# A convolution stem's gradients on one core: eight sums of raw steps of x made during the forward convolution and kept in DRAM, and one more split leaf

## The chip, the cores and the metric

The kernel runs on one core of a Trainium2 chip. Its time is the device time of one execution in microseconds (us); lower is better. TensorE (PE) multiplies, VectorE (DVE) and ScalarE (ACT) work on elements, GpSimd (POOL) sets small areas, and SyncE (SP) issues nearly all DMAs from one queue, in order. Each engine carries out its own instructions strictly in the order in which they were written down, so one that waits holds up all behind it on its engine.

## The reference, cut to what matters

```python
B, T, D, K = 2, 16000, 256, 31          # stride 2, L = 7985 output rows
h = einsum('blc,cd->bld', x[:, 0:2*L:2, :], w[0]) + ... + (the same for taps 1 to 30)
mu, var = mean and variance of h over l
out = gelu((h - mu) / sqrt(var + 1e-5) * gn_gamma + gn_beta)      # tanh form
# returned: out, and the gradients of x, w, gn_gamma, gn_beta for grad_out
```

Everything is bf16 in and out. There are three large products: the forward convolution, the gradient of x, and the gradient of w (31 taps of 256 x 256, each a sum over both batches and all 7985 rows).

## The kernel before

**Fewer multiplications by sums.** All three convolutions are split by Karatsuba's rule, several levels deep: in place of the four products of two halves with two halves, three products are made, with sums or differences of the operands, and combined afterwards. A, C_ and B_ name the first half, the second half, and their combination. DVE makes the operands' sums and differences; PE's work becomes less and DVE's more. Where the innermost level is split too, a "leaf" becomes three smaller products.

**Stages.** The order of the program is F0 and F1 (forward convolution, batch 0 and 1, `forward`), G0 and G1 (gradient of x, `input_grad`), W (gradient of w, `weight_grad`). The forward convolution of a batch takes x in four quarters c = 0 to 3; each is turned by DMA into the one buffer XT (`x_load`) and worked on in three branches, in the order B_, A, C_. `forward` is a generator: after each branch it yields (b, c, br), and the loop at the end of `conv_stem_kernel` adds other work there. In F0 that is `w2_part(c)`: a quarter of w's taps is turned by four DMA transposes into VR, five differences are made into VD, and nine stores of 256 KB put them into DRAM (vl) for the gradient of x. VR and VD lie at byte REG of the arena, 14336 bytes together. After batch 0's statistics, `gelu_batch(0, REG, ...)` takes a ring of buffers at the same place; its 16 units (`gelu_unit`, lines 947 to 986, five multiplications or additions on line 968 each) run beside F1 and have to be done before `e_comp(0, 0)` can make the input of G0.

**W.** `weight_grad` goes through nine combinations n = 0 to 8 (`COMBOS`: (A,A), (A,C), (A,B), (C,B), (B,B), (B,A), (B,C), (C,A), (C,C)) of the two outer levels. For each it needs four tiles of x (`x_tile`, 1 MB each, for two batches and two halves k3). A tile of (A,A), (A,C), (C,A) or (C,C) is one raw load; (A,B) and (B,B) are made in place from tiles that are there; (C,B), (B,A) and (B,C) each need two raw loads and one addition of 4096 elements per partition (`w_add`, line 1413). Then XSUM is made from each pair of tiles (also line 1413), a pair sum of it (`pair_x`, line 1508), differences of the gradient's tiles (`leaf_d`, line 1587; `pair_d`, line 1516), and the products: `w_pairs` and `w_single` in matmuls of 256 columns, `w_leaf` in matmuls of 512 (all on line 1447). A whole leaf is 64 matmuls of 512 columns. A leaf in the set `NODES` is split into 96 matmuls of 256 columns, for which DVE makes two pair sums, four pair differences and two PSUM additions (`w_both`, line 1540). `place` hands out the buffers for these from up to three sets; the set "late" shares its bytes with XR, the buffers of the second raw loads.

**What sets the order.** Every instruction is first only noted (`Plan.add`) with a duration and its reads and writes. `Plan.listing` then plays all engines and DMAs through and picks for each engine the instruction that is ready and has the earliest due time: that of its first user, or PE's time at its noting plus `slack`, shifted by the entry of its kind in the table `lead`. `hold` keeps an instruction back until PE has come to a given place, `look` says how far PE may pick ahead, `pads` spreads work with time to spare further from the DMAs it waits for. `PACE` gives the due times of the GELU units. The resulting order is then fixed in the program.

Lines used later: 561 (`tt` in `f_sums`), 551 (`w_sub`), 596 (`f_mm`, forward matmuls), 676 (`ve`), 680 (`ve_neg`), 1162 (`g_mm`, matmuls of the gradient of x), 1357 (`sub` in `d2_piece`), 415 and 420 (`load` and `turn`, all DMAs).

Of the kernel before, what the change touches and what calls it, by code (L numbers as in the profile page):

```python
# [11 lines left out]
BF16 = mybir.dt.bfloat16  # L12
ACT = mybir.ActivationFunctionType
ALU = mybir.AluOpType
# [6 lines left out]
A, B_, C_ = 0, 1, 2  # L21
# [17 lines left out]
class Plan:  # L39
# [3 lines left out]
    def __init__(self, tc):  # L43
# [9 lines left out]
        self.lead = {  # L53
            "F0 f_mm f_three_ac": -2.5,
            "F0 f_mm f_three_b": -4.0,
            "F0 f_mm pe_turn": 9.5,
            "F0 f_three_b f_first": 2.0,
            "F0 f_three_b forward": 2.5,
            "F0 keep f_first": 4.5,
            "F0 load load_w": -4.5,  # L60
            "F0 put x_first": -4.5,
            "F0 tt second": -1.0,
            "F0 tt third": -1.5,
            "F0 turn w2_part": 8.0,
            "F0 turn x_load": -3.5,
            "F0 ve f_first": -1.0,
            "F0 ve f_seed": -4.0,
            "F0 w_sub f_first": 2.0,
            "F1 f_mm f_leaf": -4.0,
            "F1 f_mm f_three_ac": -3.0,  # L70
            "F1 f_mm f_three_b": -9.5,
            "F1 f_three_b forward": 4.5,
            "F1 gelu_unit gelu_batch": 3.0,
            "F1 load gelu_unit": -2.0,
            "F1 tiny elem_finalize": 2.0,
            "F1 tiny fwd_stats": -11.5,
            "F1 tt f_sums": 1.5,
            "F1 tt gelu_unit": -4.0,
            "F1 tt second": -7.5,
            "F1 turn x_load": -3.0,  # L80
            "G0 e_comp conv_stem_kernel": -1.0,
            "G0 g_mm g_three_ac": 3.0,
            "G0 g_mm g_three_b": -3.0,
            "G0 g_three_b input_grad": 6.0,
            "G0 keep g_evac": -3.0,
            "G0 load dn_turn": 1.0,
            "G0 load e_load": 4.5,
            "G0 load gelu_unit": 2.0,
            "G0 load load_w2": 4.0,
            "G0 tiny elem_finalize": -8.5,  # L90
            "G0 tt first": -2.0,
            "G0 tt second": -9.0,
            "G0 turn gelu_batch": -7.0,
            "G0 w_sub load_w2": -8.0,
            "G1 e_comp conv_stem_kernel": 12.5,
            "G1 g_mm g_leaf": -4.0,
            "G1 g_mm g_outer": -1.5,
            "G1 g_mm g_three_ac": -4.0,
            "G1 keep g_evac": -10.5,
            "G1 load dn_turn": -11.5,  # L100
            "G1 load e_load": -2.5,
            "G1 load g_evac": 20.0,
            "G1 signed g_seed": -7.5,
            "G1 spread e_comp": -5.5,
            "G1 sub d2_piece": -7.5,
            "G1 tt first": 9.5,
            "G1 tt second": -5.5,
            "G1 tt third": -2.0,
            "G1 ve_neg g_seed": 11.5,
            "W keep w_keep": -2.0,  # L110
            "W keep weight_grad": 3.0,
            "W leaf_d weight_grad": -2.0,
            "W pair_x weight_grad": -1.5,
            "W turn out0_late": -7.0,
            "W ve w_done": 12.0,
            "W ve weight_grad": -3.5,
            "W w_add weight_grad": -2.0,
            "W w_add x_tile": 3.0,
            "W w_both weight_grad": 9.0,
            "W w_emit w_done": 7.5,  # L120
            "W w_mm w_leaf": -3.5,
            "W w_mm w_single": 0.5,
            "W w_pairs weight_grad": -2.5,
# [211 lines left out]
def conv_stem_kernel(  # L335
# [33 lines left out]
    dn_d = [dram.tile([NDR, D], BF16, name=f"dnd{b}") for b in range(NB)]  # L369
    pc_d = [dram.tile([P, 1024], FP32, name=f"pcd{k}") for k in range(4)]  # L370
# [1033 lines left out]
    NODES = {(0, A), (0, C_), (1, A), (1, C_), (3, A), (4, A), (6, A), (7, A), (7, C_), (8, C_)}  # L1404
# [16 lines left out]

    def x_tile(n, b, k3):
        i1, i2 = COMBOS[n]
        j = KEYS.index((b, k3))
        t = (XT_ if n % 2 else XS_)[j]
        if (i1, i2) in ((A, B_), (B_, B_)):
            w_add(t, t, XT_[j])
        else:
            ks = [(k1, k2) for k1 in raws[i1] for k2 in raws[i2]]
            x_raw(b, k3, *ks[0], t)  # L1430
            for k in ks[1:]:
                w_add(t, t, x_raw(b, k3, *k))
        return t
# [120 lines left out]
    def weight_grad():  # L1554
# [3 lines left out]
        def place(n):  # L1558
            ks = ("all",) + (("early",) if n < 2 else ()) + (("late",) if n not in (3, 5) else ())
# [98 lines left out]
    PACE = ((1385.0, 117.0), (191.0, 24.5))  # L1658
    fw = forward()
# [99 lines left out]
```

## Time and profile before

| | us |
|---|---|
| median of 3 runs | 1187.01 (1183.07 to 1188.23) |
| the profiled execution, its own time | 1189.54 |
| its span, first to last instruction | 1187.8 |
| PE busy / DVE busy / ACT busy | 1149.0 / 1047.6 / 570.0 |
| DMA queue of SP: bytes | 253.93 MB |

The profile shows one execution. "Idle before" in a group's row is the time its engine stood still just ahead of these instructions, with what ended it; in the rows in order of time the same stands in brackets. A matmul's own duration overlaps with the next one's, so PE's pace is read from stretches without a wait, not from the mean of one. The granted clock is 1.00 where PE runs at full speed. The DMA share is the mean busy share of 16 DMA engines; it can come out above 1.

### The profile page before, as it was taken

To read this page: it belongs to the slowest core of one execution; us is meant where nothing else is said; L and a number is where in the kernel's file an instruction comes from. 1 tells how busy PE (TensorE), PEld (TensorE's weight loads), DVE (VectorE), ACT (ScalarE), POOL (GpSimd) and SP (SyncE) were. 2 spreads that over 40 slices of the span, in tenths; PEclk is the share of its full clock that TensorE was granted. 3 is DMA by queue.
4 is the path that set the end of the run, shared out by engine and by line. 5 is a ranking of instruction groups with operands and counts; after the bars stand their busy time and mean duration, and the time that the engine had idled before them with its cause. 6 is when DMAs were issued, how large, how long until landed. Compare 5 with 4: busy or idle time off the path is not lost.

```text
span 1187.8 us, 19338 instructions
## 1 busy us (share of the span) xinstructions
PE 1149.0 (97%) x7739; PEld 763.5 (64%) x7796; DVE 1047.6 (88%) x1358; ACT 570.0 (48%) x873; POOL 18.9 (2%) x67
## 2 busy tenths in 40 slices
PE   5999999999999999999999999999999999989998
PEld 3888889777777964444444444444488656656685
DVE  7997898799999989999879997788889898777995
ACT  1254454788885578978884476433322212111200
POOL 0000000000000000000000000000000000000000
PEclk9999999999999999999999999999999999999999
DMA  9446949968986799567639998697998824986774
GB/s 212 73 115 122 200 121 182 205 146 204 204 209 124 270 353 252 167 225 186 221 115 292 270 329 265 161 318 266 317 235 266 271 90 151 359 300 198 239 219 140
DMA packets 334100, 255.17 MB, mean 215 GB/s; under 512 B 187500, under 2 KB 312682, under 8 KB 325738
## 3 DMA queue, kind: packets, MB, share of 16 engines
q1 hardware_dynamic: 333818, 253.93, 76.6%
q8 instruction: 61, 1.00, 0.3%
q14 instruction: 29, 0.24, 0.1%
q0 software_dynamic: 192, 0.00, 0.0%
HBM read 118.95 MB, written 89.62 MB: 176 GB/s over the span
## 4 chain that ended last, share of the span: by engine, by line
PE 46%; DVE 14%; DMA 6%; issue 4%; ACT 1%; SPq 0%; DVEq 0%; ACTq 0%
PE ps L1162 27%; PE ps L1447 15%; PE ps L596 4%; DVE arena L1413 3%; DMA arena<-in_x_dram 2%; DMA arena<-dnd 2%; DVE arena L1357 2%; DVE arena L1587 2%; DVE ps L676 1%; DVE arena L676 1%; DVE arena L1516 1%; DVE arena L1508 1%; DMA dnd<-arena 1%; DVE arena L1121 1%; DVE ps L1540 1%
## 5 line engine op out<-in xcount | busy, mean ns | idle before, releaser
L1162 PE MATMUL ps<-arena 128*128 128x512 bf16 x1974 | 429.7, 376 | 6.6 <-DVE ps L676 3.6
L596 PE MATMUL ps<-arena 128*128 128x256 bf16 (+4 forms) x3460 | 408.2, 281 | 17.8 <-DVE arena L551 7.1
L596 PEld LDWEIGHTS <-arena 128*128 128x128 bf16 x3460 | 338.1, 99 | 87.7 <-DVE arena L551 7.5
L1162 PEld LDWEIGHTS <-arena 128*128 128x128 bf16 x2016 | 197.3, 98 | 237.7 <-issue 6.8
L1447 PE MATMUL ps<-arena 128*128 128x256 bf16 (+1 forms) x2305 | 312.1, 298 | 10.5 <-DVE arena L1508 7.3
L1447 PEld LDWEIGHTS <-arena 128*128 128x128 bf16 x2320 | 228.1, 98 | 94.6 <-DVE arena L1508 8.7
L691 ACT ACTIVATE arena<-ps 128x1024 f32<-128x1024 f32 (+1 forms) x143 | 145.7, 1020 | 285.3 <-PE ps L1447 98.1
L561 DVE TENSOR_TENSOR arena<-arena 128x1087 bf16<-128x1087 bf16 (+3 forms) x211 | 175.5, 866 | 13.7 <-PE ps L596 12.4
L968 DVE TENSOR_TENSOR arena<-arena 128x1024 bf16<-128x1024 bf16 x160 | 107.0, 683 | 8.5 <-ACT arena L962 3.9
L1413 DVE TENSOR_TENSOR arena<-arena 128x4096 bf16<-128x4096 bf16 x38 | 86.3, 2284 | 20.8 <-DMA arena<-in_x_dram 19.5
L1121 DVE TENSOR_TENSOR arena<-arena 128x516 bf16<-128x516 bf16 (+3 forms) x176 | 83.6, 506 | 8.6 <-PE ps L1162 8.0
L676 DVE TENSOR_TENSOR ps<-ps,arena 128x1024 f32<-128x1024 f32 x60 | 73.1, 1224 | 7.9 <-PE ps L1447 4.5
L1357 DVE TENSOR_TENSOR arena<-arena 128x768 bf16<-128x768 bf16 (+3 forms) x112 | 65.4, 636 | 9.9 <-DMA arena<-dnd 4.7
L711 ACT ACTIVATE arena<-ps 128x512 bf16<-128x512 f32 (+1 forms) x64 | 36.9, 578 | 70.4 <-PE ps L596 67.9
L676 DVE TENSOR_TENSOR ps<-arena,ps 128x1024 f32<-128x1024 f32 x44 | 53.8, 1223 | 9.3 <-PE ps L1162 5.5
L1532 ACT COPY ps<-ps 128x256 f32<-128x256 f32 x54 | 19.3, 357 | 78.7 <-PE ps L1447 77.6
L1587 DVE TENSOR_TENSOR arena<-arena 128x2304 bf16<-128x2304 bf16 x36 | 47.4, 1348 | 4.8 <-PE ps L1447 4.8
L1516 DVE TENSOR_TENSOR arena<-arena 128x1024 bf16<-128x1024 bf16 x76 | 48.7, 682 | 1.6 <-DMA arena<-d2d 1.6
L551 DVE TENSOR_TENSOR arena<-arena 128x2048 bf16<-128x2048 bf16 (+1 forms) x52 | 49.8, 989 | 0.0
L958 DVE SCALAR_TENSOR_TENSOR arena<-arena 128x1024 bf16<-128x1024 bf16 x32 | 39.0, 1219 | 11.3 <-ACT arena L956 11.1
L1189 ACT ACTIVATE ps<-ps 128x512 f32<-128x512 f32 x48 | 27.9, 582 | 41.1 <-PE ps L1162 38.0
L1508 DVE TENSOR_TENSOR arena<-arena 128x2048 bf16<-128x2048 bf16 x38 | 45.3, 1216 | 1.2 <-PE ps L1162 1.2
(79 smaller groups left out, 632.8 us busy)
## 6 DMA issues: line engine op xcount, KB each, us to landing
arena<-in_x_dram SPq DMA_DIRECT2D x40, 1024.0 KB, 9.8
arena<-d2d SPq DMA_DIRECT2D x16, 1216.0 KB, 11.5
out_dram<-arena SPq DMA_DIRECT2D x14, 1024.0 KB, 4.4
d2d<-arena SPq DMA_DIRECT2D x30, 384.0 KB, 7.1
arena<-dnd SPq DMA_DIRECT2D x10, 960.0 KB, 5.8
vl<-arena SPq DMA_DIRECT2D x36, 256.0 KB, 3.3
arena<-vl SPq DMA_DIRECT2D x9, 1024.0 KB, 6.8
hd<-arena SPq DMA_DIRECT2D x8, 1024.0 KB, 5.0
```

The costliest lines, as they stand in the source:

```text
L561: lambda: nc.vector.tensor_tensor(out=o, in0=a, in1=b, op=ALU.add))
L596: yield nc.tensor.matmul(ps[:, dh, cs], lhsT=wt, rhs=mv, start=s0, stop=False, skip_group_check=True)
L676: add("DVE", dve(1024, 1), [out], [a, b], lambda: nc.vector.tensor_tensor(out=out, in0=a, in1=b, op=op))
L691: lambda: nc.scalar.activation(out=out, in_=ps, func=ACT.Copy, scale=scale))
L968: add("DVE", dve(1024), [o], [a, b_], lambda: V.tensor_tensor(out=o, in0=a, in1=b_, op=op))
L1121: lambda: nc.vector.tensor_tensor(out=o, in0=a, in1=b, op=ALU.add))
L1162: yield nc.tensor.matmul(ps[:, e, 0:wide], lhsT=lt, rhs=mv, start=s0, stop=False, skip_group_check=True)
L1357: lambda: nc.vector.tensor_tensor(out=out, in0=a, in1=b_, op=ALU.subtract))
L1413: add("DVE", dve(4096), [o], [a, b], lambda: nc.vector.tensor_tensor(out=o, in0=a, in1=b, op=ALU.add))
L1447: yield nc.tensor.matmul(ps[:, s, c0:c1], lhsT=lt, rhs=mv, start=s0, stop=False, skip_group_check=True)
L1516: add("DVE", dve(1024), [d4[:, j]], [d], lambda j=j, o=o, st_=st_: nc.vector.tensor_tensor(out=d4[:, j], in0=d[:, o:o + 3 * st_ + 1:st_, : ...
L1587: add("DVE", dve(2304), [DL[i3, b]], [D2[b]], lambda b=b, i3=i3, o_=o_: nc.vector.tensor_tensor(out=DL[i3, b], in0=D2[b][:, o_:o_ + 17:2, ...
```

## The change

`x_pre(b, k3, k2)` is new. It makes one of the four tiles' sums of combination 5 or 6 during F0: in four pieces it loads the two raw steps k1 = 0 and 1 side by side (512 KB), adds them (1024 elements per partition) and stores the sum (256 KB) into a DRAM tile xsd. Its two buffers take 12288 bytes at REG, where VR and VD lie. It is called eight times in F0, twice in each quarter, and each call is held until PE has come there: after branches A and C_ of quarter 0, after B_ and C_ of quarters 1 and 2, after B_ and A of quarter 3. `w2_part(c)` stays after C_, but goes to branch A in the last quarter, and stands ahead of the x_pre that shares its place.

In W, `x_tile` for combinations 5 and 6 is now one load of 1 MB from xsd: eight loads in place of sixteen raw ones, and no addition. `NODES` gains (4, C_) and (5, A) and loses (7, C_), and `place` may hand out the set "late" in combination 5 too.

In `f_first` (the first branch of the program) the differences of w and the first sums of x are written down in another order, and the second half of the first difference is made to come after the first sum. The table `lead` has new entries and values throughout, and `slack`, `look`, `pads` and `PACE` change; the long table is cut here.

```diff
@@ -46,81 +46,93 @@
-        self.slack = 70.0
+        self.slack = 50.0
         self.hold = -1
-        self.look = 13
-        self.pads = (3122.5, 3149.5, 2842.0)
+        self.look = 14
+        self.pads = (3467.0, 3517.5, 3220.5)
         self.lead = {
...
-            "F0 w_sub f_first": 2.0,
...
+            "F0 w_sub f_first": -1.0,
...
         }
@@ -367,6 +379,7 @@
     y_d = [dram.tile([D, 2048], BF16, name=f"yd{c}") for c in range(NCK)]
     NDR = 192 + 8192 + 256
     dn_d = [dram.tile([NDR, D], BF16, name=f"dnd{b}") for b in range(NB)]
+    xs_d = {(b, k3, k2): dram.tile([P, 4096], BF16, name=f"xsd{b}{k3}{k2}") for b in range(2) for k3 in range(2) for k2 in range(2)}
     pc_d = [dram.tile([P, 1024], FP32, name=f"pcd{k}") for k in range(4)]
     d2_d = [dram.tile([9, P, 19 * D], BF16, name=f"d2d{b}") for b in range(NB)]
 
@@ -546,9 +559,9 @@
             add("SP", 0.6, [gb16[:, i, :]], [], small_load, dma=0.6)
         add("DVE", 0.2, [gbf[:]], [gb16[:]], lambda: nc.vector.tensor_copy(out=gbf[:], in_=gb16[:]))
 
-    def w_sub(o, a, b):
+    def w_sub(o, a, b, *then):
         n = o.free_size()
-        add("DVE", dve(n), [o], [a, b], lambda: nc.vector.tensor_tensor(out=o, in0=a, in1=b, op=ALU.subtract))
+        add("DVE", dve(n), [o], [a, b, *then], lambda: nc.vector.tensor_tensor(out=o, in0=a, in1=b, op=ALU.subtract))
 
     def i_tap(q, par, br, lf):
         return 8 * q + par + 4 * (lf == C_) + 2 * (br == C_)
@@ -817,12 +830,13 @@
                 w_sub(WD1[br, lf], v[:, :, 1:4:2], v[:, :, 0:4:2])
 
     def f_first(xt):
-        for sl in (A, C_):
-            for ch in range(2):
-                for v in ([slice(None)] if ch or sl == C_ else [0, 1]):
-                    w_sub(*(W[br][:, sl, ch, :, v] for br in (B_, C_, A)))
         ops, third, second = f_sums(xt, 0, 0, B_, 0, [W[B_][:, A, 0, :, v] for v in range(2)])
+        w_sub(*(W[br][:, A, 0, :, 0] for br in (B_, C_, A)))
         second(A)
+        w_sub(*(W[br][:, A, 0, :, 1] for br in (B_, C_, A)), ops[A])
+        w_sub(*(W[br][:, A, 1] for br in (B_, C_, A)))
+        for ch in range(2):
+            w_sub(*(W[br][:, C_, ch] for br in (B_, C_, A)))
         second(C_)
         for br in (B_, A, C_):
             for ch in range(2):
@@ -1401,7 +1415,7 @@
     for k, o in (("early", 110720), ("late", 57344)):
         PD[k] = [(sb(o + 4096 * i, 4, 512), sb(o + 8192 + 4096 * i, 2, 4, D)) for i in range(2)]
     LATE = {0: ((0, 94336), (1, 102528)), 8: ((2, 24576), (3, 40960))}
-    NODES = {(0, A), (0, C_), (1, A), (1, C_), (3, A), (4, A), (6, A), (7, A), (7, C_), (8, C_)}
+    NODES = {(0, A), (0, C_), (1, A), (1, C_), (3, A), (4, A), (4, C_), (5, A), (6, A), (7, A), (8, C_)}
     P1 = [sb(94336 + 4096 * i, 1024, dt=FP32) for i in range(8)]
     P2 = [sb(o, 1024, dt=FP32) for o in (77824, 81920, 182016, 186112)]
     WO = [sb(202816 + 2048 * i, 2, 2, D) for i in range(3)]
@@ -1419,12 +1433,26 @@
         load(t, xblk(b)[:, :, 4 * k3 + 2 * k2 + k1, :], 1 << 20, 1024)
         return t
 
+    XP = [(sb(REG + 6144 * i, 2, 2, 512), sb(REG + 6144 * i + 4096, 2, 512)) for i in range(2)]
+
+    def x_pre(b, k3, k2):
+
+        r = 4 * k3 + 2 * k2
+        for f in range(4):
+            xp, xo = XP[f % 2]
+            load(xp, xblk(b)[:, 2 * f:2 * f + 2, r:r + 2, :], 524288, 2048)
+            add("DVE", dve(1024), [xo], [xp], lambda xp=xp, xo=xo: nc.vector.tensor_tensor(
+                out=xo, in0=xp[:, :, 0], in1=xp[:, :, 1], op=ALU.add))
+            load(xs_d[b, k3, k2][:, 1024 * f:1024 * f + 1024], xo.rearrange("p f c -> p (f c)"), 262144, 2048)
+
     def x_tile(n, b, k3):
         i1, i2 = COMBOS[n]
         j = KEYS.index((b, k3))
         t = (XT_ if n % 2 else XS_)[j]
         if (i1, i2) in ((A, B_), (B_, B_)):
             w_add(t, t, XT_[j])
+        elif i1 == B_:
+            load(t.rearrange("p f c -> p (f c)"), xs_d[b, k3, 1 if i2 == A else 0][:], 1 << 20, 4096)
         else:
             ks = [(k1, k2) for k1 in raws[i1] for k2 in raws[i2]]
             x_raw(b, k3, *ks[0], t)
@@ -1556,7 +1584,7 @@
         turn_ = [0]
 
         def place(n):
-            ks = ("all",) + (("early",) if n < 2 else ()) + (("late",) if n not in (3, 5) else ())
+            ks = ("all",) + (("early",) if n < 2 else ()) + (("late",) if n != 3 else ())
             turn_[0] += 1
             return PD[ks[(turn_[0] + 1) % len(ks)]]
 
@@ -1655,8 +1683,9 @@
 
     RINGS = ((3, 2, 2, 2), (2, 1, 1, 0))
     D2AT = {(0, 3, 0): (0, 1), (0, 3, 1): (2, 3), (1, 0, 0): (4, 5), (1, 0, 1): (6,)}
-    PACE = ((1385.0, 117.0), (191.0, 24.5))
+    PACE = ((1507.0, 111.5), (85.0, 30.5))
     fw = forward()
+    xpre = [(b_, *k_) for b_ in range(NB) for k_ in KEYS]
     add("DVE", 0.1, [JK], [], lambda: nc.vector.memset(JK, 0.0))
     for b, c, br in fw:
         if (b, c, br) == (0, 1, B_):
@@ -1666,9 +1695,14 @@
                       (dn_d[1][128:207, :], zt2[0:79]), (dn_d[0][0:15, :], zt2[0:15])):
                 load(z[0], z[1], 65536, 512, "POOL", slack=300.0)
             plan.hold = -1
-        if b == 0 and br == C_:
+        if b == 0:
             plan.hold = plan.npe
-            w2_part(c)
+            if br == (A if c == 3 else C_):
+                w2_part(c)
+            if br == (A if c == 3 else C_) or br == (B_ if c else A):
+                plan.slack = 300.0
+                x_pre(*xpre.pop(0))
+                plan.slack = 90.0
             plan.hold = -1
         if (b, c, br) == (1, 0, B_):
             plan.stage = "F1"
```

More of the change, by code (lines that the diff above doesn't have):

```diff
@@ L48, in __init__ @@
         self.pe = 0.0
[L49 removed]
+        self.slack = 50.0
         self.hold = -1
[L51 to L52 removed]
+        self.look = 14
+        self.pads = (3467.0, 3517.5, 3220.5)
         self.lead = {
[L54 removed]
+            "F0 f_evac last": -4.0,
+            "F0 f_mm f_outer": -4.0,
+            "F0 f_mm f_three_ac": -4.0,
             "F0 f_mm f_three_b": -4.0,
[L56 to L67, printed above, removed]
[L68 to L123 removed]
@@ new lines, in __init__ @@
+            "F0 f_mm pe_turn": 13.0,
+            "F0 f_outer forward": 3.5,
+            "F0 f_three_b f_first": 14.5,
+            "F0 load conv_stem_kernel": 4.0,
+            "F0 load put": 9.0,
+            "F0 load x_pre": -8.0,
+            "F0 put x_first": -8.0,
+            "F0 tt f_sums": 5.0,
+            "F0 tt second": 0.5,
+            "F0 tt third": -4.5,
+            "F0 turn x_load": -7.0,
+            "F0 ve f_first": -4.0,
+            "F0 ve f_seed": -4.5,
+            "F0 ve_neg f_seed": -5.5,
```

61 lines of the change are left out of this document (added).

## The prediction, made before the result was known

> **What bounds the kernel now.** I read the page first, then the windows by stage, then the rows of TensorE in order of time, and last what VectorE did just before each wait of TensorE.
>
> ```profile
> span 1187.8 us, 19338 instructions
> PE 1149.0 (97%) x7739; PEld 763.5 (64%) x7796; DVE 1047.6 (88%) x1358; ACT 570.0 (48%) x873; POOL 18.9 (2%) x67
> ```
>
> TensorE (PE) is busy for 1149.0 of 1187.8 us, so only two things can shorten the run: fewer columns of matmul, or part of the 38.8 us in which PE is idle. VectorE (DVE) is the next fullest. A window's row has the stretch and its length, then busy time and count of PE, PEld, DVE, ACT and POOL, the granted clock, the DMA share and GB/s.
>
> ```profile
> 64.00:215.00 151.00, 148.38 (x1383) 135.07 (x1382) 129.71 (x154) 69.06 (x159) 1.92 (x3) 1.00 0.66 146
> 215.00:290.00 75.00, 74.83 (x563) 54.72 (x562) 66.97 (x104) 60.92 (x93) 0.00 (x0) 1.00 0.86 191
> 290.00:416.00 126.00, 124.77 (x1007) 97.97 (x1005) 125.56 (x180) 89.41 (x151) 3.69 (x10) 1.00 0.80 201
> ```
>
> These rows are the forward convolution, batch 0 to about 215 us, then batch 1. DVE is idle for 21.3 us in the first, 8.0 in the second, 0.4 in the third. In the third stretch DVE has to finish the GELU units of batch 0 before the input gradient can start at 416, and there it sets the pace:
>
> ```profile
> 374.20 42.28 PE L596 MATMUL ps<-arena 128*128 128x256 bf16 x388 [1.23 <-DVE arena L561]
> ```
>
> The weight gradient (W) runs from 861 us. Its two waits below are the ones this change touches; they lie where combinations 4 (B,B), 5 (B,A) and 6 (B,C) follow each other.
>
> ```profile
> 1015.12 2.29 DVE L1413 TENSOR_TENSOR arena<-arena 128x4096 bf16<-128x4096 bf16 x1 [9.38 <-DMA arena<-in_x_dram]
> 1017.33 2.35 DVE L1540 TENSOR_TENSOR ps<-ps,arena 128x1024 f32<-128x1024 f32 x2
> 1018.61 21.40 PE L1447 MATMUL ps<-arena 128*128 128x256 bf16 x130 [1.66 <-DVE ps L1540]
> 1037.11 4.61 DVE L1413 TENSOR_TENSOR arena<-arena 128x4096 bf16<-128x4096 bf16 x2
> 1042.90 1.22 DVE L1508 TENSOR_TENSOR arena<-arena 128x2048 bf16<-128x2048 bf16 x1
> 1044.18 8.06 PE L1447 MATMUL ps<-arena 128*128 128x256 bf16 x57 [4.17 <-DVE arena L1508]
> ```
>
> Read them as one story. L1413 adds two 1 MB raw tiles of x; at 1015 it stood 9.38 us in DVE's queue for a load, and the PSUM addition queued behind it (L1540) came late, so PE waited 1.66 us. Then the same kind of additions held back L1508, the pair sum of combination 5, and PE waited 4.17 us.
>
> **The change part by part.**
>
> *1. Sums taken out of W.* Combinations 5 and 6 now load four finished tiles each, in place of eight raw ones and four additions. Eight L1413 go.
>
> ```profile
> L1413 DVE TENSOR_TENSOR arena<-arena 128x4096 bf16<-128x4096 bf16 x38 | 86.3, 2284 | 20.8 <-DMA arena<-in_x_dram 19.5 <-PE ps L1162 1.1
> arena<-in_x_dram SPq DMA_DIRECT2D x40, 1024.0 KB, 9.8
> 1020.00:1025.00 5.00, 5.00 (x48) 4.47 (x47) 1.98 (x1) 0.96 (x1) 0.00 (x0) 1.00 1.03 420
> 1040.00:1045.00 5.00, 0.83 (x6) 0.61 (x6) 4.42 (x4) 0.63 (x1) 0.00 (x0) 0.93 1.02 321
> 1045.00:1050.00 5.00, 5.00 (x35) 3.91 (x34) 4.28 (x2) 1.90 (x6) 0.00 (x0) 0.73 1.09 356
> 1006.50 1.26 SPq L415 DMA_DIRECT2D arena<-in_x_dram  x2
> ```
>
> That is 8 x 2.284 = 18.3 us of DVE and 8 MB of DMA less, just where the DMA share stands at 1.02 to 1.09. What is late next for combination 5: its last tiles can be overwritten from about 1006 (a raw load is issued there), land some 9.8 us later, and then two sums of 2.3 and two pair sums of 1.2 follow: 1006 + 10 + 7 = 1023, against 1040 when PE wants them. So I take both waits as gone: 1.66 + 4.17 = 5.8 us. The clock comes back too: after the long wait it was granted at 0.73 for 5 us, worth 5 x 0.27 = 1.4 us.
>
> A shorter wait has lowered the clock as well, in combination 3:
>
> ```profile
> 974.40 0.61 PE L1447 MATMUL ps<-arena 128*128 128x256 bf16 x4 [1.72 <-DVE arena L1508]
> 975.53 41.41 PE L1447 MATMUL ps<-arena 128*128 128x256 bf16 x298 [0.53 <-DVE arena L1508]
> 975.00:980.00 5.00, 4.47 (x27) 3.31 (x27) 5.00 (x5) 1.02 (x1) 0.00 (x0) 0.66 0.74 220
> ```
>
> Its raw sums stay, so it is not in my sum. It shows what a new wait may cost: 1.72 + 0.53 = 2.25 us, and up to 5 x 0.34 = 1.7 us of clock. The Trainium skill ("TensorE: Matmul & The Clock Gate", What's actually happening) says that the clock is halved after an idle window of about 3.4 us; the wait of 4.17 us fits that, the one of 2.25 does not, and there the measurement decides. By the page alone, a new wait of 2 us would cost no clock.
>
> *2. Split leaves.* A leaf takes 64 matmuls of 512 columns, a split one 96 of 256. Leaves (4,C) and (5,A) become split, (7,C) goes back: one more in all. The chain of waits gives the pitch, free of pipelining:
>
> ```profile
> 861.35 45.43 PE ps L1447 x416
> 1056.33 10.74 PE ps L1447 x49
> ```
>
> 45.43 / 416 = 0.109 us at 256 columns, 10.74 / 49 = 0.219 at 512. Whole: 64 x 0.219 = 14.0; split: 96 x 0.109 = 10.5. That is **-3.5 us of PE**, with nothing to hide it. The price is DVE work, two pair sums, four pair differences and two PSUM additions:
>
> ```profile
> L1508 DVE TENSOR_TENSOR arena<-arena 128x2048 bf16<-128x2048 bf16 x38 | 45.3, 1216 | 1.2 <-PE ps L1162 1.2
> L1516 DVE TENSOR_TENSOR arena<-arena 128x1024 bf16<-128x1024 bf16 x76 | 48.7, 682 | 1.6 <-DMA arena<-d2d 1.6
> L1540 DVE TENSOR_TENSOR ps<-ps,arena 128x1024 f32<-128x1024 f32 x20 | 24.0, 1224 | 4.6 <-PE ps L1447 4.6
> ```
>
> 2 x 1.216 + 4 x 0.682 + 2 x 1.224 = 7.6 us. In combinations 4 to 6 DVE so pays 15.2 and saves 18.3; in 7 it saves 7.6. It is covered; were it not, it would be rival one.
>
> *3. Sums put into the first convolution.* Eight calls of x_pre, each of four pieces: a 512 KB load, an addition of 1024 elements (as L1516, 0.682), a 256 KB store. DVE gets 32 x 0.682 = **21.8 us**, SP 64 issues, the DMA engines 24 MB. At 420 GB/s and a share of 1.03 (row 1020) the bytes need about 25.2 MB / 420 = 60 us of the engines; free are 0.34 x 151 + 0.14 x 75 = 62. So DVE and DMA are both filled nearly to the brim. DVE's idle time to 290 us is 29.3, but in small pieces; the first and the last of the 14 gaps to 215 us that are shorter than one addition:
>
> ```profile
> 76.42 1.23 DVE L676 TENSOR_TENSOR ps<-arena,ps 128x1024 f32<-128x1024 f32 x1 [0.25 <-PE ps L596]
> 200.48 1.23 DVE L680 SCALAR_TENSOR_TENSOR ps<-ps,arena 128x1024 f32<-128x1024 f32 x1 [0.47 <-PE ps L596]
> ```
>
> The 14 sum to 4.7 us; I count them as lost. In most of them DVE waits for PE, so it stands ahead of PE there, and an addition of 0.7 us in its way is not felt at once.
>
> The buffers of x_pre lie in the bytes of w2_part's raw and difference tiles, and GELU's ring takes the same bytes next. So calls of the two kinds go one after the other, and GELU starts when the last is done.
>
> ```profile
> 192.75 6.52 SPq L420 DMA_TRANSPOSE arena<-in_w_dram  x4
> 217.76 0.33 SPq L415 DMA_DIRECT2D arena<-hd  x1
> 222.11 0.43 SPq L415 DMA_DIRECT2D vl<-arena  x1
> arena<-in_w_dram SPq DMA_TRANSPOSE x16, 3.9
> vl<-arena SPq DMA_DIRECT2D x36, 256.0 KB, 3.3
> arena<-hd SPq DMA_DIRECT2D x32, 256.0 KB, 3.9
> arena<-pcd SPq DMA_DIRECT2D x4, 512.0 KB, 6.9
> ```
>
> Now the bytes are handed over at about 217 to 222. A 512 KB load lies between 3.9 us (256 KB here) and 6.9 (512 KB in W); I take the middle, 5.4. With two buffers a piece takes (5.4 + 0.7) / 2 = 3.0, a call 12, eight calls 97. A w2_part needs about 6.5 + 3.9 + 3.4 (five differences) + 9 stores of 0.4 to issue + 3.3 = 21, packed to 18 where steps overlap; four make 72. The first call is held until PE is through the second branch of the first quarter; four quarters fill 215 us, so that is at about 56, the start included. 56 + 97 + 72 = 225: some **8 us later** than now; ends: 3.9 and 18 give 201 (no delay), 6.9 and 29 (192.75 to 222.11) give 293 (70 late). GELU gives DVE 16 units of at least 5 x 0.683 + 1.22 + 1.22 = 5.9 us, from the first to the last of these:
>
> ```profile
> 229.56 1.22 DVE L958 SCALAR_TENSOR_TENSOR arena<-arena 128x1024 bf16<-128x1024 bf16 x1
> 371.01 1.22 DVE L980 CUSTOM_DVE_ANT_0 arena<-arena 128x1024 bf16<-128x1024 bf16 x1
> L968 DVE TENSOR_TENSOR arena<-arena 128x1024 bf16<-128x1024 bf16 x160 | 107.0, 683 | 8.5 <-ACT arena L962 3.9 <-ACT arena L960 3.6
> ```
>
> That is 94 us of 143, so 0.7 us of DVE work is put off for each us of delay: 5.6. Sum: 21.8 + 5.6 + 4.7 - 29.3 = 2.8 us that DVE cannot place, which PE feels in the third stretch: **+3 us**. Ends: 0 (DVE's lead takes it up) and 21.8 (no gap usable).
>
> On SP, a store that waits for its addition holds back what is queued behind it, the transposes of x and w above all; the same pattern cost SP up to 5.1 us at once elsewhere:
>
> ```profile
> SPq L415 <- DVE arena L1357: 73.4, 41, 5.1
> ```
>
> I take it at nothing, since x is turned more than a branch ahead; without that cover it is part of rival two. POOL issues none of this.
>
> The Trainium skill ("DMA: Bandwidth & Descriptors", Bandwidth) speaks against pieces under 1 MB, being far from peak; its fit for one DMA (2.0 us plus bytes / 436 GB/s, section Anatomy of one DMA) would give a 512 KB load an estimated 3.2 us, so eight calls take 8 x 4 x 1.95 = 62 us and the delay vanishes, which makes the term 0 and lies inside the forecast's own range. No run here shows such a load yet.
>
> *4. Order at the start, leads, pads, look, paces.* They change order only. f_first fixes subtraction, sum, subtraction; the four instructions ahead of the first forward matmul stay the same: 0, ends -0.7 and +3.9 (the six sums that the subtractions now precede). Elsewhere in the forward part a better order could win 2.6 + 0.2 + 1.2 = 4.0 us of PE idle (three windows above); I take 0, and as much the other way.
>
> *Sum:* -5.8 - 1.4 - 3.5 + 3 = **-7.7 us**. The profiled execution took 1189.5 (span 1187.8 and 1.7 around it), 2.5 above the median of 1187.0; both move by it, to 1181.8 and **1179.3**.
>
> **Rivals.** *One, the gain in W is taken by a new wait:* 15 us of split-leaf work now stand in combinations 4 and 5, and a wait like that at 974 (2.25 plus 1.7 of clock) appears once or twice. For it:
>
> ```profile
> 960.00:990.00 30.00, 27.70 (x204) 20.44 (x203) 29.95 (x26) 4.19 (x8) 0.00 (x0) 0.94 0.28 84
> ```
>
> DVE has no idle time in the 30 us before. Against: the margin above, 1040 - 1023 = 17 us. Then 5.8 + 1.4 shrink to about 1: 1187 - 1 - 3.5 + 3 = 1185.5, within 0.5%.
>
> *Two, slower: the shared bytes are handed over late.* If x_pre and w2_part wait for each other as long as now (DMA full, SP blocked by a store), GELU of batch 0 starts d late, and PE waits 21.8 + 0.7 d + 4.7 - 29.3 before 416. It outweighs W's 10.7 from d = 19; with 5.4 kept and w2_part at 26, d is 40, PE waits 25 us: 1187 - 10.7 + 25 = 1201. For it: no DVE slack after 290; against: w2_part's stores lie far apart now because nobody wants them.
>
> *Three, the change doesn't do what it says:* the sums come too late from DRAM. Written before 300, read after 990; I give it nothing.
>
> **How the numbers follow.** Forecast 0.55 (own range 1173 to 1183), rival one 0.25, rival two 0.20. A measurement of this kernel tells about 0.5% (5.9 us: 1181.1 to 1192.9) from no change. Of the forecast 0.48 lies below 1181.1 and 0.07 within; of rival one 0.02 and 0.23; of rival two 0.03 within and 0.17 above. Faster 0.50, same 0.33, slower 0.17. The range takes in rival one and most of rival two: 1171 to 1198.
>
> **What would show it.** Right: L1413 30 times, L1447 with one leaf's shift from 512 to 256 columns, no PE wait above 1 us and a clock of 1.00 between combinations 4 and 6, DVE over 95% busy from 64 to 215, the first GELU load by 230, the input gradient starting within 4 us of 416. Wrong: PE waits for DVE between 290 and 416 of over 6 us in sum, or a new wait for L1508, L1540 or L1587 in W.

## The result, and the profile after

The changed kernel takes **1195.11 us** (median of 4 runs, 1193.88 to 1196.58), the kernel before 1186.42 in the same comparison (4 runs, 1183.07 to 1188.23). The ratio is 1.0078, 95% interval 1.0061 to 1.0096: **slower by 0.8%**, where 1179.3 was forecast.

The page first, as it was read before:

```profile
span 1193.4 us, 19604 instructions
PE 1150.4 (96%) x7828; PEld 768.1 (64%) x7828; DVE 1054.3 (88%) x1390; ACT 571.2 (48%) x873; POOL 21.5 (2%) x67
```

PE's busy time in sum says little here: the trace of before holds 7739 matmuls beside 7796 weight loads (page of before), that of after 7828 beside 7828, so some matmuls of before seem to have no record. The rows of PE in order of time show where the time went. Lines have moved: 609 is the forward matmul, 1176 that of the gradient of x, 1475 that of W.

```profile
155.47 9.80 PE L609 MATMUL ps<-arena 128*128 128x256 bf16 x88 [2.29 <-DVE ps L689]
168.97 17.03 PE L609 MATMUL ps<-arena 128*128 128x256 bf16 x148 [3.69 <-DVE ps L689]
186.54 32.36 PE L609 MATMUL ps<-arena 128*128 128x256 bf16 x318 [0.55 <-ACT arena L724]
...
324.03 6.26 PE L609 MATMUL ps<-arena 128*128 128x512 bf16 x40 [0.49 <-DVE arena L574]
...
883.13 304.74 PE L1475 MATMUL ps<-arena 128*128 128x256 bf16 x2352
```

The last row is the whole of W: 304.74 us without one wait. In before W took 322.6 us (from 861.2 to 1183.8). So **W won 17.9 us**, more than the 10.7 that were forecast. But it begins at 883.13 instead of 861.2: **21.9 us are lost ahead of it**, and the last stores end 5.5 us after W instead of 4.0. 21.9 + 1.5 - 17.9 = 5.5; the spans differ by 5.6. The medians differ by more (1195.11 - 1186.42 = 8.7), since the profiled execution of before took 1189.54, 3.1 above its median here.

The windows of the forward convolution, to be held against the three rows of before (columns as there):

```profile
64.00:215.00 151.00, 142.30 (x1307) 128.36 (x1305) 133.80 (x167) 64.94 (x151) 1.40 (x2) 0.99 0.95 248
215.00:290.00 75.00, 72.00 (x561) 54.44 (x560) 58.96 (x89) 49.28 (x81) 0.53 (x1) 1.00 0.94 225
290.00:416.00 126.00, 121.05 (x901) 89.23 (x900) 123.88 (x173) 95.08 (x153) 3.13 (x5) 0.97 0.77 178
```

The reader is to see three things. PE now loses 8.7 us in the first stretch, where it lost 2.6. The DMA share has gone from 0.66 to 0.95. And DVE, though about 14 of the 22 us of additions belong here (x3_add below), is busy for 133.80 us, only 4 more than before: it stands, and has done 167 instructions there where x3_add has done 175. What it stands for:

```profile
DVE arena L1444 <- DMA xsd<-arena: 17.5, 13, 2.7
DVE arena L564 <- DMA xsd<-arena: 3.5, 1, 3.5
```

(Total, times, longest.) L1444 is x_pre's addition; it waits until the store of the sum before last has left its buffer. How this reaches PE, in order of time:

```profile
155.46 0.52 SPq L428 DMA_DIRECT2D arena<-in_x_dram  x1
...
156.03 0.47 SPq L428 DMA_DIRECT2D xsd<-arena  x1
156.53 3.76 SPq L433 DMA_TRANSPOSE arena<-in_x_dram  x1
...
160.97 0.47 SPq L428 DMA_DIRECT2D xsd<-arena  x1
...
161.48 3.93 SPq L433 DMA_TRANSPOSE arena<-in_x_dram  x1
...
167.08 0.69 DVE L1444 TENSOR_TENSOR arena<-arena 128x1024 bf16<-128x1024 bf16 x1 [2.68 <-DMA xsd<-arena]
167.69 1.22 DVE L689 TENSOR_TENSOR ps<-ps,arena 128x1024 f32<-128x1024 f32 x1
...
168.97 1.44 PE L609 MATMUL ps<-arena 128*128 128x256 bf16 x6 [3.69 <-DVE ps L689]
```

On SP, x_pre's loads and stores alternate with the transposes of x; each of the two transposes shown holds the queue for about 4 us. The addition at 167.08 stood 2.68 us for a store, the addition into PSUM (L689) stood behind it in DVE's queue, and PE, which needed that one, waited 3.69 us.

### The profile page after: what moved, and what is told of

Same layout as the page of the kernel before. It is cut to its first block, busy times and chain, and to the rows that moved or that the text cites. A ratio compares the mean times of both kernels' runs of the same rounds, so it can differ in the third digit from the quotient of the medians.

```text
span 1193.4 us, 19604 instructions
## 1 busy us (share of the span) xinstructions
PE 1150.4 (96%) x7828; PEld 768.1 (64%) x7828; DVE 1054.3 (88%) x1390; ACT 571.2 (48%) x873; POOL 21.5 (2%) x67
## 4 chain that ended last, share of the span: by engine, by line
PE 70%; DVE 14%; SPq 5%; DMA 4%; issue 4%; ACT 2%; DVEq 0%; ACTq 0%
PE ps L1176 30%; PE ps L1475 26%; PE ps L609 15%; DVE arena L574 3%; SPq L433 3%; DVE arena L982 2%; DMA xsd<-arena 2%; SPq L428 2%; DVE ps L689 2%; DVE arena L564 1%; DVE arena L1371 1%; DVE arena L972 1%; DMA out_dram<-arena 1%; DVE arena L994 1%; DVE arena L689 1%
## 5 line engine op out<-in xcount | busy, mean ns | idle before, releaser
L609 PE MATMUL ps<-arena 128*128 128x256 bf16 (+4 forms) x3460 | 414.4, 283 | 33.4 <-DVE arena L564 9.1
L1176 PE MATMUL ps<-arena 128*128 128x512 bf16 (+1 forms) x2016 | 431.6, 376 | 4.1 <-DVE ps L689 3.3
L609 PEld LDWEIGHTS <-arena 128*128 128x128 bf16 x3460 | 340.5, 99 | 106.9 <-issue 17.9
L1475 PE MATMUL ps<-arena 128*128 128x256 bf16 (+1 forms) x2352 | 304.7, 293 | 0.0
L574 DVE TENSOR_TENSOR arena<-arena 128x1088 bf16<-128x1088 bf16 (+3 forms) x211 | 176.2, 866 | 6.0 <-PE ps L609 4.6
L689 DVE TENSOR_TENSOR ps<-ps,arena 128x1024 f32<-128x1024 f32 x60 | 73.1, 1223 | 5.5 <-PE ps L1475 3.2
L1427 DVE TENSOR_TENSOR arena<-arena 128x4096 bf16<-128x4096 bf16 x30 | 67.9, 2283 | 4.5 <-PE ps L1475 3.3
L689 DVE TENSOR_TENSOR ps<-arena,ps 128x1024 f32<-128x1024 f32 x44 | 53.8, 1223 | 5.3 <-PE ps L1176 5.0
L1536 DVE TENSOR_TENSOR arena<-arena 128x2048 bf16<-128x2048 bf16 x40 | 47.7, 1216 | 1.3 <-PE ps L1176 1.2
L972 DVE SCALAR_TENSOR_TENSOR arena<-arena 128x1024 bf16<-128x1024 bf16 x32 | 39.0, 1219 | 10.4 <-ACT arena L970 7.6
```

The costliest lines, as they stand in the source:

```text
L609: yield nc.tensor.matmul(ps[:, dh, cs], lhsT=wt, rhs=mv, start=s0, stop=False, skip_group_check=True)
L689: add("DVE", dve(1024, 1), [out], [a, b], lambda: nc.vector.tensor_tensor(out=out, in0=a, in1=b, op=op))
L1176: yield nc.tensor.matmul(ps[:, e, 0:wide], lhsT=lt, rhs=mv, start=s0, stop=False, skip_group_check=True)
L1427: add("DVE", dve(4096), [o], [a, b], lambda: nc.vector.tensor_tensor(out=o, in0=a, in1=b, op=ALU.add))
L1475: yield nc.tensor.matmul(ps[:, s, c0:c1], lhsT=lt, rhs=mv, start=s0, stop=False, skip_group_check=True)
```

## The experiments

The first question was what in x_pre costs the time: its additions (no room on DVE), its transfers, or the coupling of both, in which DVE's queue stands for SP's. A second question came out of the first run. In most of these kernels, combinations 5 and 6 load something else than the kept sum; each text says so. The ratio is to the kernel before, measured on the same chip in the same comparison.

| run | what is left of x_pre in F | us (lowest to highest) | ratio to before (95%) |
|---|---|---|---|
| x1_none | nothing, order kept | 1181.84 (1180.97 to 1182.93) | 0.9961 (0.9946 to 0.9975) |
| x3_add | additions | 1183.26 (1181.27 to 1184.95) | 0.9974 (0.9964 to 0.9984) |
| x4_nostore | loads, additions | 1184.76 (1180.96 to 1186.70) | 0.9984 (0.9970 to 0.9999) |
| x10_quarter_store | loads, additions, 2 of 8 MB of stores | 1184.38 (1181.23 to 1186.77) | 0.9983 (0.9971 to 0.9996) |
| x13_bytes_alone | all transfers, no other engine waits for their data | 1191.41 (1190.53 to 1194.04) | 1.0043 (1.0027 to 1.0060) |
| the change | all | 1195.11 (1193.88 to 1196.58) | 1.0078 (1.0061 to 1.0096) |
| x2_dma | all transfers, chained | 1241.49 (1240.63 to 1245.68) | 1.0474 (1.0445 to 1.0503) |

### Without x_pre

```diff
 x_pre: the load, the addition and the store are planned, but not issued
 x_tile, combinations 5 and 6:
-    load(t, xs_d[b, k3, k2])
+    load(t, one raw step of x)
```

> The changed kernel with its written order kept, but the 96 instructions of x_pre (32 loads, 32 additions, 32 stores) left out; combinations 5 and 6 load 1 MB of raw x in place of the sums, so the gradient of w is not the reference's. It tells what x_pre costs in all. If x_pre is the whole cause of the loss in the forward part (883.1 - 861.2 = 21.9 us later start of W), the time is about 1195 - 22 = 1173 us and GELU's first load is back near 218 us. If the new leads and the moved w2_part are the cause, it stays above 1190.

Measured: 1181.84. x_pre as a whole so costs **13.3 us**; but the rest did not come down as far as expected. The window and the rows of PE:

```profile
64.00:215.00 151.00, 148.72 (x1387) 135.44 (x1386) 127.60 (x152) 70.53 (x165) 1.86 (x3) 1.00 0.61 136
```
```profile
177.28 85.90 PE L611 MATMUL ps<-arena 128*128 128x256 bf16 x732 [0.55 <-ACT arena L726]
...
311.37 18.91 PE L611 MATMUL ps<-arena 128*128 128x512 bf16 x134 [2.15 <-DVE arena L576]
...
869.91 75.25 PE L1483 MATMUL ps<-arena 128*128 128x256 bf16 x679
```

To 215 us PE loses no more than in before. W begins at 869.9: of the 21.9 us, x_pre made 13.2 and the order of everything else 8.7. The last quarter of F0 begins at 177.28 here and at 186.54 in after, so 9.3 of the 13 us fall before that point.

### Additions alone; loads and additions; transfers alone in a chain

```diff
 x3_add:     no load, no store; the addition reads resident weights
 x4_nostore: no store
 x2_dma:     no addition
-    store(xs_d, xo)
+    store(xs_d, half of xp, as loaded)      # waits for the load, the next load waits for it
```

> The same written order with x_pre's 32 additions alone: they read resident weights, no load and no store is made, and combinations 5 and 6 load raw x, so the gradient of w is not the reference's. Theory 3 (no room on VectorE) expects most of the loss to stay, 1185 to 1195; theories 1 and 2 expect 1173 to 1178, as 21.8 us of additions then fall into 29 us of idle time.

> The same written order with x_pre's loads and additions but without its 32 stores; combinations 5 and 6 load raw x, so the gradient of w is not the reference's. An addition then waits for its own load alone. Theory 1 expects the waits of L1444 (17.5 us in 13 waits in the changed kernel) gone and 1174 to 1180; theory 3 expects 1185 or more; theory 2 expects part of the delay to stay, since the loads and the transposes are still in SP's queue.

> The same written order with x_pre's loads and stores, but without its 32 additions on VectorE: each store takes half of the loaded bytes as they are, so the gradient of w is not the reference's. Theory 1 (VectorE stands in its queue at an addition until the store of two pieces before has landed, and what is behind it comes late) and theory 3 (VectorE has no room for 21.8 us of additions) both expect the loss gone: 1173 to 1178. Theory 2 (GELU's bytes are handed over some 30 us late because of the chain of transfers) expects the hand-over still late and 1187 or more.

The windows of the first two, x3_add and then x4_nostore:

```profile
64.00:215.00 151.00, 148.72 (x1388) 135.44 (x1386) 141.98 (x175) 69.69 (x163) 1.92 (x3) 1.00 0.63 144
```
```profile
64.00:215.00 151.00, 148.72 (x1388) 135.45 (x1386) 139.60 (x174) 70.42 (x165) 1.93 (x3) 1.00 0.89 221
```

DVE takes the additions, 14.4 us of them in this stretch (141.98 against 127.60), and PE does not lose 0.1 us: the theory that DVE has no room falls. With the 16 MB of loads, PE's row is still the same; only with the stores does it change. By medians: additions 1.4 us, loads 1.5 more, the stores 10.4 more.

x2_dma took over 60 us more than two of the theories expected. Its store waits for its load and the next load but one for that store, all in SP's queue. The transposes of x behind them came late, and DVE, without one addition of x_pre, stood for them (x2_dma's waits, as above):

```profile
DVE arena L576 <- DMA arena<-in_x_dram: 37.7, 6, 9.5
```

So it showed that the transfers can cost time without the additions, but by a chain that the change does not have. x13_bytes_alone, below, is the clean form of it.

### More buffers, another queue

If SP's queue or the distance of two buffers were the cause, a third output buffer in the same bytes, or stores issued elsewhere, should take the cost away. All three kernels here are whole and keep the order.

```diff
 x7_three_kept:
-    XP: 2 x (load 4096 + sum 2048 bytes)
+    2 loads of 4096, 3 sums of 2048 bytes
 x8_pool:            -    nc.sync.dma_start(xs_d, xo)
                     +    nc.gpsimd.dma_start(xs_d, xo)
 x11_all_by_gpsimd:  the loads of x_pre by nc.gpsimd as well
```

> The changed kernel, whole, in its own written order; only x_pre's output buffers are three in place of two (in the same 14336 bytes), so an addition waits for the store of three pieces before. If the loss is VectorE standing at an addition for the store of two pieces before (17.5 us in 13 waits), most of the 10 to 13 us between the kernels with and without stores comes back: W begins at 869 to 873, 1182 to 1186 us, L1444's waits below 4 us. If the stores cost by what they do to SP's queue and the DMA engines (bytes, backlog), W begins above 878 and the time stays above 1190.

> The changed kernel, whole, in its own written order; only x_pre's 32 stores are issued by GpSimd in place of SP, so SP does not stand at a store that waits for its addition, and a store does not stand behind the transposes of x on SP. If SP's queue is what makes the stores late, the time is 1182 to 1187 us. If the stores land late for another reason, VectorE still waits and it stays above 1190.

> Whole: the order of after is kept, but all 64 of x_pre's DMAs, loads and stores, are issued by GpSimd (busy 1.4 us of 151 in 64 to 215), so that SP's queue holds what it held in before, and a load that waits for its buffer holds nothing else. The stores alone by GpSimd gave 1194.3 us. Theory Q (x_pre's pieces and x_load's transposes hold each other up in SP's one queue): 1184 to 1187 us, W starts at 868 to 873 us, and DVE waits under 5 us in all for x_pre's loads and stores. Theory B (the DMA engines themselves are full, whoever issues): 1191 to 1195 us, W starts at 880 us or later, the additions still wait 13 us or more for loads and stores.

Measured: x7_three_kept 1192.48 us (1191.13 to 1195.02; ratio 1.0047, 1.0025 to 1.0068), x8_pool 1194.27 (1193.86 to 1194.83; 1.0069, 1.0052 to 1.0086), x11_all_by_gpsimd 1215.42 (1211.97 to 1220.01; 1.0246, 1.0217 to 1.0276). DVE's waits, of x7 (the addition is L1504) and of x8:

```profile
DVE arena L1504 <- DMA arena<-in_x_dram: 18.0, 13, 3.7
```
```profile
DVE arena L1444 <- DMA arena<-in_x_dram: 10.0, 8, 2.6
DVE arena L1444 <- DMA xsd<-arena: 5.0, 5, 1.8
```

With three buffers the store is no longer waited for, but the same 18 us are now waited for the load; with the stores on GpSimd, 15. The wait moves to the next transfer: neither a third buffer (2.6 us less than the change) nor another queue for the stores (0.8 less) takes the cost away. The Trainium skill ("DMA: Bandwidth & Descriptors", Issuing engines are not separate DMA queues) says that DMAs of all issuing engines run on the same 16 DMA engines, and that another issuer saves only the issue time. x8 agrees (1194.27 against 1195.11). x11 goes beyond it: the theory that expected 1184 to 1187 falls, but so does the 1191 to 1195 of the other. The transfers between 51 and 260 us (KB each, median us to landing), of after and of x11; the row of q0, which holds what GpSimd issues, has packets, MB and the share of the 16 engines' time:

```profile
arena<-in_x_dram SPq DMA_DIRECT2D x29, 512.0 KB, 4.9
...
xsd<-arena SPq DMA_DIRECT2D x32, 256.0 KB, 5.2
...
arena<-in_x_dram SPq DMA_TRANSPOSE x17, 7.2
```
```profile
q0 software_dynamic: 6114, 21.47, 34.4%
...
arena<-in_x_dram SPq DMA_TRANSPOSE x15, 10.5
```

With x_pre's bytes in GpSimd's queue, the transposes of x take 10.5 us to land instead of 7.2, x_pre's additions wait 28.6 us for their stores instead of 17.5, and W begins at 906.3 instead of 883.1. From 64 to 215 us GpSimd is busy for 26.89 us instead of 1.40, and its queue too stands for the additions (113.1 us in 18 waits between 30 and 300). Which of these makes the loss, and why the transposes land so late, was not tried.

### The bytes

```diff
 x10_quarter_store:
-    store(xs_d[..., 1024 columns], xo)
+    store(xs_d[...,  256 columns], xo)
 x13_bytes_alone: no addition; loads go round three buffers;
-    store(xs_d, xo)
+    store(xs_d, resident weights)
```

> The order of after is kept; each of the 32 stores of x_pre writes 256 of its 1024 columns (2 MB in all instead of 8), and combinations 5 and 6 load the raw block instead of the kept sum, so the output is not the reference's. The two runs between which this one stands: all stores 1195.1 us, no stores 1184.8 us. Theory B (bytes: the DMA engines have no room left in 64 to 215 us, where the DMA share is 0.95): three quarters of the stores' bytes go, so 1186 to 1188 us. Theory Q (the place in SP's queue: a store is issued behind a transpose that holds SP for 4 to 5 us, and two buffers later the addition waits for it, whatever its size): 1192 to 1195 us, W starts at 880 us or later, and the additions still wait over 10 us for the stores.

> The order of after is kept; x_pre's 32 loads and 32 stores are issued at their places with all their bytes (24 MB), but the additions are left out, each store reads a part of the weights that is resident already, and the loads go round three buffers, so no instruction of any engine but SP waits for any of them; combinations 5 and 6 load the raw block, so the output is not the reference's. Theory B (the bytes slow the transfers that F needs, x_load's transposes above all): 1189 to 1196 us, W starts at 875 us or later, though DVE has 22 us less to do than in after. Theory S (the bytes cost only because DVE's additions stand in its queue for them): 1181 to 1185 us, as without x_pre (1181.8), W starts at 868 to 872 us.

x10_quarter_store has every load, addition, store, wait and issue of the change, and 18 MB instead of 24. It took 1184.38, even less than the 1186 to 1188 of theory B and no more than x4 without any store (1184.76). Its window and DVE's waits for the stores (17.5 us in after):

```profile
64.00:215.00 151.00, 148.72 (x1388) 135.39 (x1386) 138.91 (x173) 69.93 (x163) 1.92 (x3) 1.00 0.93 230
```
```profile
DVE arena L1446 <- DMA xsd<-arena: 6.0, 6, 2.0
```

x13_bytes_alone has all the bytes, and no engine but SP waits for one of them. It took 1191.41, as theory B expected. Its windows and rows of PE:

```profile
64.00:215.00 151.00, 148.44 (x1384) 135.04 (x1382) 123.50 (x147) 70.37 (x165) 1.92 (x3) 1.00 0.97 256
215.00:290.00 75.00, 68.88 (x502) 49.13 (x500) 56.15 (x86) 48.00 (x73) 0.00 (x0) 0.98 0.83 209
```
```profile
261.98 49.85 PE L611 MATMUL ps<-arena 128*128 128x256 bf16 x360 [4.27 <-ACT arena L726]
...
318.95 11.26 PE L611 MATMUL ps<-arena 128*128 128x512 bf16 x74 [2.15 <-DVE arena L576]
```

Here PE loses no more before 215 than in x1. The backlog comes out at the change of batch, where PE waits 4.27 us, and by 319 PE is 7.6 us behind x1 (318.95 against 311.37). The rows ahead of that wait show its path:

```profile
243.78 0.94 SPq L430 DMA_DIRECT2D arena<-hd  x2
...
249.81 1.24 ACT L972 ACTIVATE arena<-arena,stats 128x1024 bf16<-128x1024 bf16 x1 [8.28 <-DMA arena<-hd]
...
252.21 1.23 DVE L974 SCALAR_TENSOR_TENSOR arena<-arena 128x1024 bf16<-128x1024 bf16 x1 [11.24 <-ACT arena L970]
```

GELU's first load is issued at 243.78, in x1 at 228.52: in SP's queue it stands behind x_pre's last transfers and the transposes among them. ACT stood 8.28 us in its queue for it and DVE 11.24 us for ACT, and what PE needs of both came late. In after 9.3 of the 13 us are lost earlier, while DVE stands at x_pre's additions. So the bytes cost the time by two different paths: the last 6 of the 24 MB cost 10.7 us with the additions (from x10 to after), and all 24 cost 9.6 without them (from x1 to x13). That leaves some 4 of the 13.3 us to the additions and to DVE's standing for the transfers; whether the second path would take over in the change if DVE did not stand is not shown. (x10 also has shorter rows, 512 bytes per partition instead of 2048; the count of rows is the same.) Between 18 MB (share 0.93) and 24 (0.95 to 0.97) the transfers fall behind; where in between was not measured.

### The order: 8.7 us that x_pre did not make

```diff
 x5_unplanned:  x_pre left out before the order is made; 5 and 6 load a raw step
 x12_old_leads: the same, and
-    lead = the new table for F0, F1, G0, G1
+    lead = the table of before for F0, F1, G0, G1
```

> The changed kernel with x_pre left out before the order is made, so that the planner gives its place to other work; combinations 5 and 6 load raw x, so the gradient of w is not the reference's. With x_pre left out afterwards (order kept) W began at 869.9 us, 8.7 us later than in the kernel before. If those 8.7 us were planned for x_pre (GELU put later because its bytes come free later), W begins at 861 to 863 and the time is about 1174 us. If they come from the new leads and the moved w2_part, W begins near 870 and the time is about 1182.

> As x5_unplanned (after without x_pre, which is left out before the order is made; combinations 5 and 6 load the raw block instead of the kept sum, so the output is not the reference's), but the leads of the stages F0, F1, G0 and G1 are those of before; W keeps the leads of after, and f_first, the place of w2_part and the split leaf stay as in after. x5_unplanned began the input gradient's long run of matmuls at 440.2 us and took 1182.1 us; before began it at 428.9 us. Theory L (the new leads make the later order of F1 and its hand-over to G0): the long run begins at 428 to 432 us, and the time is below x5's by most of these 10 us, 1172 to 1178 us, if G1's own order does not give some of it back. Theory M (the moved subtractions and the moved part of the transposed weights make it): 437 to 442 us and 1180 to 1184 us.

x5_unplanned took 1182.06 us (1179.83 to 1184.60; ratio 0.9961, 0.9946 to 0.9976), the same as x1: the 8.7 us are not room kept for x_pre. x12_old_leads took 1194.23 (1192.38 to 1195.41; 1.0059, 1.0041 to 1.0078). The start of the long run of the gradient of x in x5, then in x12, with x12's last rows ahead of W:

```profile
440.16 19.81 PE L1176 MATMUL ps<-arena 128*128 128x512 bf16 x92 [0.67 <-DVE arena L1135]
```
```profile
431.23 29.11 PE L1167 MATMUL ps<-arena 128*128 128x512 bf16 x132
...
874.90 4.00 PE L1167 MATMUL ps<-arena 128*128 128x512 bf16 x9 [6.26 <-DVE ps L680]
...
882.90 17.30 PE L1469 MATMUL ps<-arena 128*128 128x256 bf16 x157
```

Theory L was right on F1: with the old leads, PE is at the gradient of x at 431.23, as good as the 428.89 of before. The time was missed by far, since G then lost more than was won: W begins at 882.90, in x5 at 872.20. PE's groups of G, between 440 and 890 us, of x5 and x12 (idle before them in the third part):

```profile
L1176 PE MATMUL ps<-arena 128*128 128x512 bf16 (+1 forms) x1968 | 427.5, 376 | 5.3 <-DVE ps L689 2.4 <-DVE arena L1135 0.7
```
```profile
L1167 PE MATMUL ps<-arena 128*128 128x512 bf16 x1922 | 425.2, 381 | 18.2 <-DVE ps L680 7.2 <-ACT arena L1086 4.0 <-ACT arena L695 3.6
```

18.2 us of waits instead of 5.3 (in before 6.4): the old leads don't suit G as it now stands, and in sum x12 is 12.2 us slower than x5. So the 8.7 us are not simply to be had back. Which entries of the table cost F its 9 us, and why G loses with the old ones, stays open.

### W without the second raw loads

```diff
 the kernel before, order kept; combinations 5 and 6:
-    load the second raw step; w_add
+    (neither is issued)
```

> The kernel before in its own written order, but without the eight second raw loads and eight additions of combinations 5 and 6, so the gradient of w is not the reference's. It tells what taking the sums out of W is worth by itself: the prediction's step 1 expects 5.8 us of waits and 1.4 us of clock, 1179 us. If more of W's 17.9 us comes from the sums, 1175 or less; if the gain hangs on the new leads and leaves, 1183 or more.

Measured: 1180.81 us (1177.99 to 1186.38), ratio 0.9958 (0.9943 to 0.9973). PE in W:

```profile
860.54 63.48 PE L1452 MATMUL ps<-arena 128*128 128x256 bf16 x580
...
1034.88 51.82 PE L1452 MATMUL ps<-arena 128*128 128x256 bf16 x344 [2.15 <-DVE arena L1513]
...
1150.14 22.71 PE L1452 MATMUL ps<-arena 128*128 128x512 bf16 x142 [0.37 <-DVE ps L678]
```

The sums and loads alone are worth 5.6 us by the medians. This is also the most that the idea could bring with W's old order, if the sums cost nothing elsewhere: they would have to be made in F for less than 5.6 us.

No whole kernel among the runs beats the one before. x1, x3, x5 and x9 are 0.3 to 0.4% faster, x4 and x10 less than 0.2%, and all of them leave work out.

## Why the prediction was wrong, step by step

**Step 1, sums out of W: right.** L1427 (L1413 of before) stands 30 times, as foretold, and both waits are gone. Forecast -7.2; x9 gives -5.6 by medians. In x9 2.15 of the 4.17 us stay (row 1034.88), so the sums alone don't take that wait away; in after W's new order and leaves are there too.

**Step 2, split leaf: right in size.** W of x9 runs from 860.54 to 1172.85; less its waits (3.4 us in sum) that is 308.9, against 304.7 in after: 4.2 us, of which up to 1.7 may be the clock after the wait of 2.15. Forecast -3.5. That W's other waits of before went too (3.9 us in sum, those at 974 among them) was not in the sum; rival one, a new wait there, did not come.

**Step 3, sums in F0: this step failed.** It gave +3; x_pre costs 13.3. The count of additions was right, but they cost nearly nothing (x3: 1.4). What failed is the sentence about the bytes (25.2 MB / 420 = 60 us needed, 62 free): the rate was taken from a window of 1 MB loads in W, and filling the DMA engines "nearly to the brim" was given no price. Between x1 and x13 the rate in 64 to 215 rises by 120 GB/s for 0.36 of the share. By this estimate the added transfers run at 120 / 0.36 = 333 GB/s, and 25.2 MB need 76 us, not 60. Between 51 and 260 us, where x_pre's transfers lie, the share is 0.68 in x1, which leaves 0.32 x 209 = 67 us, and 0.98 in after. "I take it at nothing, since x is turned more than a branch ahead" held only as long as the transfers kept up. And DVE was not over 95% busy from 64 to 215 but 133.80 / 151 = 89%: the time was there, and DVE stood in it. The 512 KB loads landed in 4.9 us (forecast 5.4), so the piece itself was well sized. The fit of the Trainium skill ("DMA: Bandwidth & Descriptors", Anatomy of one DMA), which it gives for DMAs issued by GpSimd, makes an estimated 3.2 us of such a load. Neither these loads of SP met it nor those that GpSimd issued in x11 (5.8 us); both run beside the transposes, but no run shows that this is the reason.

**The late hand-over (rival two) was seen, and its price was wrong.** The first GELU load of after:

```profile
249.33 0.88 SPq L428 DMA_DIRECT2D arena<-hd  x2
```

It came at 249.33 instead of 217.76, d = 31.6, for which rival two's formula gives 19 us, and so a time of 1187 - 10.7 + 19 = 1195.3. That this is what was measured is luck: PE's waits between 290 and 416 in after are 5.0 us, below the 6 that were to count as wrong, 8.7 us of the loss come from the order, and 9.3 of x_pre's 13 are lost by 186 us, before any GELU. The range of 1171 to 1198 holds the measured time through this rival alone. A late hand-over does cost, but otherwise than the formula has it. In x10 the load came 10.8 us later than in x1 (239.32), and PE was only 1.6 us later at its last wait there (313.01 against 311.37). In x13 it came 15.3 us later, and PE was 7.6 us later, through the queues of ACT and DVE at 250 to 262. So rival two had the right sign, but neither the path nor the price.

**Step 4, order at 0: failed.** x1 shows 8.7 us, and with "as much the other way" the text had allowed 4.0. x12 puts it down to the new leads: with them the gradient of x begins some 9 us later (440.16 in x5, 431.23 in x12), though with the old ones G then loses more.

Together: order 8.7, x_pre 13.2, W -17.9, the end 1.5: +5.5, as between the two profiled executions. By the medians x1 is 4.2 us below before (1181.84 against 1186.06) though its W begins 8.7 us later, so W and the end win about 13 us there, where the profiles give 16.4; that the medians' difference, 8.7, has the figure of the order's loss is chance.

## What to carry to other kernels

Price transfers that go into a stretch of another kind at the rate of that stretch, and where in-order queues stand for transfers, don't price a stretch that they nearly fill at nothing: here 18 MB more (share 0.93) cost 2.5 us, additions included, and 24 (0.95) cost 13.3. An in-order engine that is given one more small instruction waiting for a DMA passes the DMA's lateness on to all behind it, so look at what stands next in its queue rather than at its idle time. When the order comes from a tuned table, a change of the table is a change with a price of its own, and a run with the new order and without the new work shows it.

## What was not expected of the hardware

A DMA transpose of x issued by SP held SP's queue itself: 3.8 and 3.9 us in the rows of after above (DMA share 0.95), against 0.5 for a plain transfer; in before, at 0.66, four in a row took 10.68 us (from 130.59), 2.7 each, and two took 6.85 (from 178.14), 3.4 each. The same 512 and 256 KB transfers, moved from SP's queue to GpSimd's, made the transposes that stayed on SP land in 10.5 us instead of 7.2 and the kernel 20.3 us slower (1215.42 against 1195.11).
